# Chunked attention feeding a mixture of experts: the transpose of the later tiles' attention weights moved from TensorE to VectorE and ScalarE

## The chip, the cores and the metric

One core of a Trainium2 chip runs the program. The time is device microseconds of one execution, and the time of a kernel is the median of its runs; lower is better.

## The reference, cut to what matters

Attention works within chunks of 64 tokens, head by head; its output is the input of four experts, whose outputs are added with normalized weights.

```python
q_c, k_c, v_c = (a.reshape(B, H, nc, 64, 64) for a in (q, k, v))     # B = H = 8, S = 576
scores = np.matmul(q_c, k_c.transpose(0, 1, 2, 4, 3)) / 8
attn = np.exp(scores - np.max(scores, axis=-1, keepdims=True))
attn = attn / (np.sum(attn, axis=-1, keepdims=True) + 1e-09)
x = np.matmul(attn, v_c)            # to (4608 tokens, 512)
p = domain_probs / (domain_probs.sum(-1, keepdims=True) + 1e-09)
for e in range(4):
    out += p[:, e:e + 1] * (np.maximum(x @ w1[e], 0.0) @ w2[e])      # 512 -> 1024 -> 512
```

Everything is in float32.

## The kernel before, in words

The 4608 tokens are 36 tiles of 128. The first four tiles form a block of their own (startup, then the plain passes); the other 32 form four pairs of 512-token blocks, eight tiles to a pair. The experts are worked in eight passes (four experts by two halves of the hidden layer): a plain pass over the first block, then passes over the first pair, then "later passes" over the other pairs. The big products split each float32 operand into a high and a low part and add three products (L465, 512 columns a matmul); for the pairs a scheme with seven instead of eight block products saves some of them, at the price of sums of blocks (Factors, Tokens, Scaled). In a later pass the hidden products (g and h) and the output products (a and b of the pass before) are woven in the order of WOVEN, L1181.

The attention of a later tile is worked beside these products, some passes before its block is needed. One tile is 128 tokens: two chunks c by eight heads. Its steps are:
- a_scores (L135): 16 matmuls of 64x64 into psa, two PSUM banks that belong to attention alone. TensorE's array has four quadrants (64 rows by 64 columns); the chunk c sets the half of the rows, the head's parity the half of the columns, and the loop of quarters (L125) goes round all four.
- a_softmax (L145): VectorE takes the maximum and subtracts it (L185, L187), ScalarE takes exp (L190).
- a_weights (L149): VectorE sums, inverts and multiplies (L193 to L198) into e in SBUF.
- a_transpose (L156): TensorE transposes e in four matmuls of 128x128 (L160) into bank 0 of psa, and one ScalarE copy brings it to pt in SBUF (L162).
- a_values (L164): 16 matmuls of 64x64 with v as weights and pt streamed (L169), into the other half of psa.
- a_copy (L174): ScalarE copies the result into xraw (L178).

a_next (L218) issues a tile's values, then the next tile's scores, the copy, and the loads of the next v and of q and k after it; v_in and qk_in have one buffer each, so a load waits until TensorE has read the old one.

When a step is issued is set by hand. For the first pair, the generator attention (L200) yields a step at a time and Beside (L1005) spreads the steps evenly over the products of the plain passes; for the second pair over those of the first pair's passes. In the plain passes an idle step stands between weights and transpose (rest = 1), so there are 41 steps for a pair there, and 33 for the second pair. For the last two pairs, attend (L1197) adds the steps after given products of WOVEN: places EARLY (6, 9, 11) or LATE (17, 21, 24) for weights, transpose and a_next, by the table TILES, five EARLY and three LATE tiles to a pair. deferred (L504) holds work that issue (L1022) emits after the next product. Each engine works its instructions in the order of issue.

The startup has its own functions for its four tiles; they don't change.

Of the kernel before, what the change touches and what calls it, by code (L numbers as in the profile page):

```python
# [8 lines left out]
F32 = mybir.dt.float32  # L9
# [6 lines left out]
P = 128  # L16
C = 64
SUB = 512
NT = SUB // P
HG = 4  # L20
GT = 2
NK = 4
# [2 lines left out]
WAITS = {"loads": 6, "softmax": 6, "copy": 3}  # L25
PAIR = 2
N_RAW = 6


@with_exitstack  # L30
def chunk_attention_moe(ctx: ExitStack, tc: tile.TileContext, qk, v, v0, dp, w1, w2, out):
# [10 lines left out]
    nc = tc.nc  # L42
# [3 lines left out]
    n_pass = 2 * n_exp  # L46
# [5 lines left out]
    att = ctx.enter_context(tc.tile_pool(name="att", bufs=1))  # L52
# [54 lines left out]

    st = {}  # L110
    xraw = {}

# [7 lines left out]
    def a_load_v(t):  # L120
        s = st[t]
        s["v"] = load.tile([P, 2 * HG, C], F32, name="v_in")
        nc.sync.dma_start(out=s["v"], in_=v[t - NT])

    def quarters():  # L125
        for j in range(HG):
            for c in range(2):
                for odd in range(2):
                    yield j, slice(c * C, (c + 1) * C), c, slice(odd * C, (odd + 1) * C), odd

    def blocks(i):

        return psa[:, :, i * HG * C : (i + 1) * HG * C].rearrange("p c (j k) -> p c j k", k=C)

    def a_scores(t):  # L135
        s = st[t]
        s["sc"] = blocks(0)
        for j, rows, c, half, odd in quarters():
            g, h = divmod(2 * j + odd, HG)
            nc.tensor.matmul(  # L140
                s["sc"][half, c, j], lhsT=s["x"][rows, g, 0, h], rhs=s["x"][rows, g, 1, h],
                start=True, stop=True,
            )

    def a_softmax(t):  # L145
        less_max(st[t]["sc"])
# [2 lines left out]
    def a_weights(t):  # L149

        s = st[t]
        s["e"] = att.tile([P, HG, 2, C], F32, name="e")
        z = psa[:, 0, HG * C : HG * C + 2 * HG].rearrange("p (c j) -> p c j", c=2)
        a_norm(s["e"].rearrange("p j c k -> p c j k"), s["sc"], z)

    def a_transpose(t):  # L156
        s = st[t]
        ps = psa[:, 0].rearrange("p (j q) -> p j q", q=P)
        for j in range(HG):
            nc.tensor.transpose(ps[:, j], s["e"][:, j].rearrange("p c k -> p (c k)"), ident)  # L160
        s["pt"] = att.tile([P, HG, P], F32, name="pt")
        nc.scalar.copy(out=s["pt"], in_=ps)  # L162

    def a_values(t):  # L164

        s = st.pop(t)
        av = blocks(1)
        for j, rows, c, half, odd in quarters():
            nc.tensor.matmul(  # L169
                av[half, c, j], lhsT=s["v"][rows, 2 * j + odd], rhs=s["pt"][rows, j, half],  # L170
                start=True, stop=True,
            )

    def a_copy(t):  # L174
        pair, i = divmod(t - NT, PAIR * NT)
        if i == 0:
            xraw[pair] = xpool.tile([P, NK, PAIR * SUB], F32, name="xraw")
        nc.scalar.copy(  # L178
            out=xraw[pair][:, :, i * P : (i + 1) * P].rearrange("p j (c q) -> p c j q", c=2), in_=blocks(1)
        )  # L180


    def less_max(a):
# [13 lines left out]
        r = r.unsqueeze(len(a.shape) - 1).broadcast_to(a.shape)  # L197
        nc.vector.tensor_tensor(out=e, in0=a, in1=r, op=ALU.mult)  # L198

    def attention(pair, rest):  # L200

        first = (1 + pair * PAIR) * NT
        last = first + PAIR * NT
        a_load(first)
        yield
        a_next(None, first)
        for t in range(first, last):  # L210
            for step in (a_softmax, a_weights, *(rest * [None]), a_transpose):
                yield
                if step:
                    step(t)
            yield
            a_next(t, t + 1 if t + 1 < last else None)
# [287 lines left out]
    deferred = []  # L504
# [274 lines left out]
        s, j = divmod(i, NT)  # L779
        nc.tensor.transpose(out_ps, acc[pair + 1, m + NK * s][:, j * P : (j + 1) * P], ident)  # L780

    B = 32

    def put_out(pair, m, s, stage):

        t = (1 + pair * PAIR + s) * SUB
# [218 lines left out]
    class Beside:  # L1005


        def __init__(self, pair, n, rest):
            self.steps = attention(pair, rest)
            self.rate, self.due = ((4 + rest) * PAIR * NT + 1) / n, 0.5  # L1010

        def load(self):

# [183 lines left out]
    def attend(at, pair, places, i):  # L1197
        t = (1 + pair * PAIR) * NT + i
        after = t + 1 if i + 1 < PAIR * NT else None
        if i == 0:  # L1200
            add(at, 13, lambda: a_next(None, t))
            add(at, 14, lambda: a_softmax(t))
        add(at, places[0], lambda: a_weights(t))
        add(at, places[1], lambda: a_transpose(t))
        add(at, places[2], lambda: a_next(t, after))
        if after:
            add(at, places[2] + 1, lambda: a_softmax(after))
# [182 lines left out]
        by_halves(steps["b"])  # L1390

    with tc.manual_schedule():
        beside = [Beside(0, (n_pass - 3) * 2 * NK, 1), Beside(1, (n_pass - 1) * 26 - 4, 0)]
# [57 lines left out]
```

## Time and profile before

| what | value |
|---|---|
| median of 3 runs | 1506.08 us (1505.98 to 1506.42) |
| the profiled execution | 1506.8 us |
| its span, first to last instruction | 1504.9 us |
| TensorE busy | 1497.4 us (100%) |
| VectorE busy | 927.9 us (62%) |
| ScalarE busy | 564.2 us (37%) |
| GpSimd busy | 871.6 us (58%) |
| SyncE's DMA queue | 65.4% of 16 engines' span |

PE is TensorE's matmuls, PEld its weight loads, DVE is VectorE, ACT ScalarE, POOL GpSimd, SP the engine that issues the DMAs. A row of a timeline gives the start, the duration, the engine, the source line, the operation, what it writes and reads, and a count of merged instructions; in brackets the idle time before it and who ended it. Matmuls are pipelined, so their durations overlap: the time that one takes from the stream is read from start to start.

### The profile page before, as it was taken

The page shows a single profiled execution, that of the slowest core. Times are in us where ns is not written, and L with a number is a line of the kernel's source. Part 1 is how long each engine was busy: PE and PEld are TensorE (multiplying, and loading weights), DVE is VectorE, ACT ScalarE, POOL GpSimd, SP SyncE. Part 2 cuts the span into 40 slices and gives each one's busy share as a digit, 9 for nine tenths or more (in the row PEclk, how much of TensorE's full clock was granted, in tenths as well). Part 3 has the DMA queues.
Part 4 walks back from the last instruction along what each step waited for, and adds up shares of the span by engine and source line. Part 5 has one row for each costly group of instructions (what it writes and reads, how often), then busy time and mean ns, then how long its engine had stood idle before and what let it go on. Part 6 is the DMA issues. An engine that isn't in the chain of part 4 may idle for free.

```text
span 1504.9 us, 23273 instructions
## 1 busy us (share of the span) xinstructions
PE 1497.4 (100%) x8779; PEld 1231.3 (82%) x8779; DVE 927.9 (62%) x1306; ACT 564.2 (37%) x983; POOL 871.6 (58%) x666
## 2 busy tenths in 40 slices
PE   9999999999999999999999999999999999999998
PEld 7888888888888888888888888888888888888887
DVE  5453554445444466666776886667667966666666
ACT  3343444344444334333333434333333433323322
POOL 2443577677757616555565755555557655555555
PEclk9999999999999999999999999999999999999999
DMA  6353349886767576666675779666666696666665
GB/s 198 127 156 124 110 152 313 275 272 217 240 232 237 197 266 218 223 211 217 201 221 186 218 204 284 204 222 218 206 198 199 188 232 233 198 199 201 202 195 155
DMA packets 197775, 314.16 MB, mean 209 GB/s; under 512 B 53776, under 2 KB 113952, under 8 KB 197664
## 3 DMA queue, kind: packets, MB, share of 16 engines
q1 hardware_dynamic: 197664, 312.68, 65.4%
q8 instruction: 69, 1.13, 0.3%
q14 instruction: 42, 0.34, 0.1%
HBM read 244.39 MB, written 68.23 MB: 208 GB/s over the span
## 4 chain that ended last, share of the span: by engine, by line
PE 99%; DMA 0%; SPq 0%; DVE 0%; ACT 0%; issue 0%
PE A L465 49%; PE C L465 29%; PE B L465 16%; PE psa L169 1%; PE psa L140 1%; PE psa L160 1%; DMA xraw<-in_qk 0%; PE C L906 0%; PE B L857 0%; PE A L837 0%; SPq L821 0%; PE A L857 0%; PE B L843 0%; PE psa L837 0%; PE psa L843 0%; PE C L1357 0%
## 5 line engine op out<-in xcount | busy, mean ns | idle before, releaser
L647 POOL TENSOR_TENSOR hfl<-wraw,hfh 128x512 fp32r<-128x512 f32 x288 | 374.3, 1315 | 211.3 <-ACT hfh L644 209.5
L465 PE MATMUL A<-xh,wf 128*128 128x512 f32 (+1 forms) x1104 | 379.3, 389 | 0.0
L465 PE MATMUL A<-hfh,wf 128*128 128x512 f32 (+1 forms) x768 | 270.0, 393 | 0.0
L644 ACT CAST hfh<-wraw 128x512 fp32r<-128x512 f32 x288 | 176.5, 622 | 212.2 <-DVE wraw L638 60.7
L465 PEld LDWEIGHTS A<-xh,wf 128*128 128x128 f32 x1104 | 206.8, 188 | 43.3
L527 ACT COPY s<-A 128x512 f32<-128x512 f32 x192 | 112.9, 588 | 328.9 <-PE A L465 328.0
L465 PE MATMUL A<-xl,wf 128*128 128x512 f32 (+1 forms) x552 | 213.7, 388 | 0.0
L465 PE MATMUL C<-xh,wf 128*128 128x512 f32 (+1 forms) x600 | 203.9, 388 | 0.7 <-ACT xh L278 0.7
L465 PEld LDWEIGHTS A<-hfh,wf 128*128 128x128 f32 x768 | 144.1, 188 | 31.2 <-DVE acc L694 1.2
L694 DVE TENSOR_TENSOR acc<-A,acc 128x512 f32<-128x512 f32 x174 | 118.9, 684 | 72.0 <-PE A L465 71.5
L465 PE MATMUL A<-hfl,wf 128*128 128x512 f32 x384 | 149.4, 389 | 0.0
L465 PE MATMUL C<-hfh,wf 128*128 128x512 f32 x384 | 133.7, 389 | 0.0
L281 POOL TENSOR_TENSOR hfl<-wraw,hfh 128x512 fp32r<-128x512 f32 x64 | 85.9, 1370 | 80.3 <-ACT hfh L278 80.3
L465 PEld LDWEIGHTS C<-xh,wf 128*128 128x128 f32 x600 | 111.5, 188 | 23.8 <-ACT xh L278 0.8
L465 PE MATMUL B<-xh,wf 128*128 128x512 f32 (+1 forms) x376 | 125.2, 384 | 0.0
L281 POOL TENSOR_TENSOR wf<-wraw,wf 128x512 fp32r<-128x512 f32 x70 | 91.5, 1328 | 54.7 <-ACT wf L278 54.5
L465 PEld LDWEIGHTS A<-xl,wf 128*128 128x128 f32 x552 | 103.5, 188 | 21.0
L465 PE MATMUL C<-xl,wf 128*128 128x512 f32 (+1 forms) x300 | 114.7, 385 | 0.0
L638 POOL TENSOR_TENSOR wf<-wraw,wf 128x512 f32<-128x512 f32 x23 | 29.7, 1292 | 144.4 <-DVE wf L632 144.4
L694 DVE TENSOR_TENSOR acc<-C,acc 128x512 f32<-128x512 f32 x90 | 62.2, 691 | 52.9 <-PE C L465 47.3
L647 POOL TENSOR_TENSOR hfl<-wf,hfh 128x512 fp32r<-128x512 f32 x48 | 71.2, 1483 | 37.0 <-ACT hfh L644 36.7
L465 PEld LDWEIGHTS C<-hfh,wf 128*128 128x128 f32 x384 | 72.1, 188 | 15.0
(186 smaller groups left out, 2710.0 us busy)
## 6 DMA issues: line engine op xcount, KB each, us to landing
wf<-w SPq DMA_DIRECT2D x336, 512.0 KB, 4.2
wraw<-in_w SPq DMA_DIRECT2D x128, 256.0 KB, 3.9
w<-wf SPq DMA_DIRECT2D x112, 256.0 KB, 4.7
qk_in<-in_qk SPq DMA_DIRECT2D x32, 512.0 KB, 5.4
v_in<-in_v SPq DMA_DIRECT2D x32, 256.0 KB, 4.5
w<-hfl SPq DMA_DIRECT2D x32, 256.0 KB, 2.7
w<-hfh SPq DMA_DIRECT2D x32, 256.0 KB, 2.9
w<-hfh SPq DMA_DIRECT2D x48, 128.0 KB, 2.7
```

The costliest lines, as they stand in the source:

```text
L140: nc.tensor.matmul(s["sc"][half, c, j], lhsT=s["x"][rows, g, 0, h], rhs=s["x"][rows, g, 1, h], start=True, stop=True,)
L160: nc.tensor.transpose(ps[:, j], s["e"][:, j].rearrange("p c k -> p (c k)"), ident)
L169: nc.tensor.matmul(av[half, c, j], lhsT=s["v"][rows, 2 * j + odd], rhs=s["pt"][rows, j, half], start=True, stop=True,)
L281: eng.tensor_tensor(out=t[1], in0=src, in1=t[0].bitcast(F32), op=ALU.subtract)
L465: nc.tensor.matmul(out, lhsT=lhs(k, a), rhs=rhs(k, b), start=first and i == 0, stop=last and i == len(parts) - 1, skip_group_check=not (fi ...
L527: nc.scalar.copy(out=t, in_=self.a)
L638: (eng or nc.vector).tensor_tensor(out=self.values[place, k], in0=self.values[a, k], in1=self.values[b, k], op=op)
L644: nc.scalar.copy(out=self.part(name, 0)[:, k], in_=self.values[name, k])
L647: (eng or nc.gpsimd).tensor_tensor(out=self.part(name, 1)[:, k], in0=self.values[name, k], in1=self.part(name, 0)[:, k].bitcast(F32), op=A ...
L694: nc.vector.tensor_tensor(out=acc[key], in0=src, in1=acc[key], op=ALU.add)
```

## The change

The weights of a later tile are no longer transposed by TensorE. VectorE's transpose works on blocks of 32x32 and leaves every block in its place, so a 64x64 matrix comes out with its four blocks transposed one by one and the two off the diagonal in each other's place. a_transpose is now this one instruction, from e to the place in PSUM where the scores stood. A new step, a_place, brings it to pt: one ScalarE copy of everything, then four copies that each move blocks of 32 partitions from the other 32 partitions of the same half.

The scores are laid out for it. The weights of a head must end in the half of the partitions in which its values' matmul wants them, so the output half of a score matmul is now that of its later use (half), with heads assigned by c ^ half; v is loaded in three transfers instead of one, the second and third with the halves of the tokens swapped; the output copy becomes two, one of them with the two banks exchanged. In quarters the innermost loop is now the half: for scores it is the half of the columns, for values that of the rows.

In the plain passes the transpose is issued together with the weights, and the placing in the step after, through deferred, behind that step's product; an empty step follows. In the first pair's passes transpose and placing are steps of their own, so both pairs now have 41 steps. In attend, the transpose follows the weights at places[0], and the placing has the transpose's old place.

```diff
 def a_load_v(t):
-    nc.sync.dma_start(out=s["v"], in_=v[t - NT])
+    to, of = (a.rearrange("p (g i h) d -> p g i (h d)", g=2, i=2) for a in (s["v"], v[t - NT]))
+    nc.sync.dma_start(out=to[:, :, 0], in_=of[:, :, 0])
+    for half in range(2):
+        rows, other = slice(half * C, (half + 1) * C), slice((1 - half) * C, (2 - half) * C)
+        nc.sync.dma_start(out=to[rows, :, 1], in_=of[other, :, 1])
 def quarters():
-    for j in range(HG):
-        for c in range(2):
-            for odd in range(2):
-                yield j, slice(c * C, (c + 1) * C), c, slice(odd * C, (odd + 1) * C), odd
+    for g in range(2):
+        for c in range(2):
+            for odd in range(2):
+                for half in range(2):
+                    yield c, half, 2 * g + odd, HG * g + 2 * (c ^ half) + odd
 def a_scores(t):
-    s["sc"][half, c, j], lhsT=s["x"][rows, g, 0, h], rhs=s["x"][rows, g, 1, h],
+    q, k = (s["x"][of_half(c), head // HG, x, head % HG] for x in range(2))
+    nc.tensor.matmul(s["sc"][of_half(half), c, slot], lhsT=q, rhs=k, start=True, stop=True)
 def a_transpose(t):
-    ps = psa[:, 0].rearrange("p (j q) -> p j q", q=P)
-    for j in range(HG):
-        nc.tensor.transpose(ps[:, j], s["e"][:, j].rearrange("p c k -> p (c k)"), ident)
-    s["pt"] = att.tile([P, HG, P], F32, name="pt")
-    nc.scalar.copy(out=s["pt"], in_=ps)
+    nc.vector.transpose(st[t]["sc"], st[t]["e"])
+def a_place(t):
+    s["pt"] = att.tile([P, 2, HG, C], F32, name="pt")
+    nc.scalar.copy(out=s["pt"], in_=s["sc"])
+    for half in range(2):
+        for i in range(2):
+            here, there = (slice(half * C + k * B, half * C + (k + 1) * B) for k in (i, 1 - i))
+            nc.scalar.copy(
+                out=s["pt"][there, :, :, i * B : (i + 1) * B],
+                in_=s["sc"][here, :, :, (1 - i) * B : (2 - i) * B],
+            )
 def a_values(t):
-    av[half, c, j], lhsT=s["v"][rows, 2 * j + odd], rhs=s["pt"][rows, j, half],
+    av[of_half(slot % 2), half, head // 2], lhsT=s["v"][of_half(half), head],
+    rhs=s["pt"][of_half(half), c, slot], start=True, stop=True,
 def a_copy(t):
-    nc.scalar.copy(out=xraw..., in_=blocks(1))
+    nc.scalar.copy(out=to[:, :, 0::2], in_=av[:, :, 0::2])
+    nc.scalar.copy(out=to[:, :, 1::2], in_=av[:, ::-1, 1::2])
 def attention(pair, close):
-    for step in (a_softmax, a_weights, *(rest * [None]), a_transpose):
+    if close:
+        steps = (a_softmax,), (a_weights, a_transpose), (lambda t: deferred.append(lambda: a_place(t)),), ()
+    else:
+        steps = (a_softmax,), (a_weights,), (a_transpose,), (a_place,)
 class Beside:
-    self.rate, self.due = ((4 + rest) * PAIR * NT + 1) / n, 0.5
+    self.rate, self.due = (5 * PAIR * NT + 1) / n, 0.5
 def attend(at, pair, places, i):
-    add(at, places[0], lambda: a_weights(t))
-    add(at, places[1], lambda: a_transpose(t))
+    add(at, places[0], lambda: a_weights(t), lambda: a_transpose(t))
+    add(at, places[1], lambda: a_place(t))
```

ScalarE's order at the first tile that the plain passes work, before (pt is the transposed weights, psa attention's PSUM banks, hfh a hidden part, wf a split weight):

```order
L278 CAST wf_825<-wraw 128x2x256
L162 COPY pt<-psa 128x512
L278 CAST wf_848<-wraw 128x2x256
L278 CAST wf_851<-wraw 128x2x256
L178 COPY xraw<-psa 128x2x4x64
```

And after:

```order
L497 ACTIVATE hfh_796<-B_813 128x512
L175 COPY pt<-psa 128x512
L179 COPY pt<-psa 32x8x32 x4
L303 CAST wf_834<-wraw 128x2x256
L303 CAST wf_851<-wraw 128x2x256
L303 CAST wf_854<-wraw 128x2x256
L200 COPY xraw<-psa 128x2x2x64
L201 COPY xraw<-psa 128x2x2x64
```

Five copies stand where one stood, and one weight split earlier, right behind the hidden part's activation; the output copy is two.

PE's order at an early tile of a later pass, before (the last products of g7, then a7, g4 and a_next):

```order
L465 MATMUL A_6150<-xh_5427,wf_6134 128x512
L160 MATMUL psa<-ident,e 128x128 x4
L465 MATMUL A_6141<-hfh_6029,wf_6109 128x512
...
L465 MATMUL A_6150<-xl_5505,wf_6134 128x512
L465 MATMUL A_6150<-xh_5504,wf_6134 128x512
L169 MATMUL psa<-pt,v_in 64x64 x16
L140 MATMUL psa<-qk_in 64x64 x16
```

And after:

```order
L490 MATMUL A_6220<-xh_5491,wf_6204 128x512
L490 MATMUL A_6211<-hfh_6096,wf_6179 128x512
...
L490 MATMUL A_6220<-xl_5569,wf_6204 128x512
L490 MATMUL A_6220<-xh_5568,wf_6204 128x512
L189 MATMUL psa<-pt,v_in 64x64 x16
L154 MATMUL psa<-qk_in 64x64 x16
```

The four transposes are gone; values and scores stand where they stood. On ScalarE the placing follows the same copy of A as the copy to pt did:

```order
L552 COPY s_6319<-A_6220 128x512
L175 COPY pt<-psa 128x512
L179 COPY pt<-psa 32x8x32 x4
L200 COPY xraw<-psa 128x2x2x64
L201 COPY xraw<-psa 128x2x2x64
```

No other instruction has come between that copy and the output's.

More of the change, by code (lines that the diff above doesn't have):

```diff
@@ L27 @@
 N_RAW = 6
+B = 32
 @with_exitstack
@@ L122, in a_load_v, with of_half @@
         s["v"] = load.tile([P, 2 * HG, C], F32, name="v_in")
-        nc.sync.dma_start(out=s["v"], in_=v[t - NT])
+        to, of = (
+            a.rearrange("p (g i h) d -> p g i (h d)", g=2, i=2) for a in (s["v"], v[t - NT])
+        )
[3 more added lines that the diff above has]
+            nc.sync.dma_start(out=to[rows, :, 1], in_=of[other, :, 1])
     def quarters():
-        for j in range(HG):
+        for g in range(2):
             for c in range(2):
                 for odd in range(2):
-                    yield j, slice(c * C, (c + 1) * C), c, slice(odd * C, (odd + 1) * C), odd
+                    for half in range(2):
+                        yield c, half, 2 * g + odd, HG * g + 2 * (c ^ half) + odd
+    def of_half(i):
+        return slice(i * C, (i + 1) * C)
     def blocks(i):
@@ L137, in a_scores @@
         s["sc"] = blocks(0)
-        for j, rows, c, half, odd in quarters():
-            g, h = divmod(2 * j + odd, HG)
-            nc.tensor.matmul(
-                s["sc"][half, c, j], lhsT=s["x"][rows, g, 0, h], rhs=s["x"][rows, g, 1, h],
-                start=True, stop=True,
-            )
+        for c, half, slot, head in quarters():
+            q, k = (s["x"][of_half(c), head // HG, x, head % HG] for x in range(2))
+            nc.tensor.matmul(s["sc"][of_half(half), c, slot], lhsT=q, rhs=k, start=True, stop=True)
     def a_softmax(t):
@@ L167, in a_values @@
         av = blocks(1)
-        for j, rows, c, half, odd in quarters():
+        for c, half, slot, head in quarters():
             nc.tensor.matmul(
-                av[half, c, j], lhsT=s["v"][rows, 2 * j + odd], rhs=s["pt"][rows, j, half],
-                start=True, stop=True,
+                av[of_half(slot % 2), half, head // 2], lhsT=s["v"][of_half(half), head],
+                rhs=s["pt"][of_half(half), c, slot], start=True, stop=True,
             )
@@ L177, in a_copy @@
             xraw[pair] = xpool.tile([P, NK, PAIR * SUB], F32, name="xraw")
-        nc.scalar.copy(
-            out=xraw[pair][:, :, i * P : (i + 1) * P].rearrange("p j (c q) -> p c j q", c=2), in_=blocks(1)
-        )
+        to = xraw[pair][:, :, i * P : (i + 1) * P].rearrange("p j (c q) -> p c j q", c=2)
+        av = blocks(1)
+        nc.scalar.copy(out=to[:, :, 0::2], in_=av[:, :, 0::2])
+        nc.scalar.copy(out=to[:, :, 1::2], in_=av[:, ::-1, 1::2])
     def less_max(a):
@@ L198, in a_norm, with attention @@
         nc.vector.tensor_tensor(out=e, in0=a, in1=r, op=ALU.mult)
-    def attention(pair, rest):
+    def attention(pair, close):
         first = (1 + pair * PAIR) * NT
@@ L210, in attention @@
         for t in range(first, last):
-            for step in (a_softmax, a_weights, *(rest * [None]), a_transpose):
+            if close:
+                steps = (a_softmax,), (a_weights, a_transpose), (lambda t: deferred.append(lambda: a_place(t)),), ()
+            else:
+                steps = (a_softmax,), (a_weights,), (a_transpose,), (a_place,)
+            for some in steps:
                 yield
-                if step:
+                for step in some:
                     step(t)
@@ L1005, in chunk_attention_moe, with __init__ @@
     class Beside:
-        def __init__(self, pair, n, rest):
-            self.steps = attention(pair, rest)
-            self.rate, self.due = ((4 + rest) * PAIR * NT + 1) / n, 0.5
+        def __init__(self, pair, n, close):
+            self.steps = attention(pair, close)
+            self.rate, self.due = (5 * PAIR * NT + 1) / n, 0.5
         def load(self):
```

9 lines of the change are left out of this document (5 added, 4 removed).

## The prediction

> **What bounds the kernel now.** I read the page first: the busy times, the clock and the chain that ended last.
>
> ```profile
> PE 1497.4 (100%) x8779; PEld 1231.3 (82%) x8779; DVE 927.9 (62%) x1306; ACT 564.2 (37%) x983; POOL 871.6 (58%) x666
> ...
> PEclk9999999999999999999999999999999999999999
> ...
> PE 99%; DMA 0%; SPq 0%; DVE 0%; ACT 0%; issue 0%
> ```
>
> TensorE (PE) is the chain, 99% of it, at a full clock; all other engines have idle time. So a microsecond taken from PE's stream is a microsecond of the span as long as nothing that PE waits for comes late, and work added elsewhere costs nothing unless it makes PE wait. A busy PE may hide stalls, so I read its timeline at the first transposed tile.
>
> ```profile
> 55.27 0.61 PE L465 MATMUL B<-xh,wf 128*128 128x512 f32 x2
> 55.72 0.39 PE L465 MATMUL B<-xl,wf 128*128 128x512 f32 x1
> 55.95 0.40 PE L465 MATMUL B<-xh,wf 128*128 128x512 f32 x1
> 56.18 0.60 PE L160 MATMUL psa<-ident,e 128*128 128x128 f32 x4
> 56.54 0.48 PE L465 MATMUL C<-hfh,hfh 128*128 128x512 f32 x1
> 56.85 0.40 PE L465 MATMUL C<-hfl,hfh 128*128 128x512 f32 x1
> ```
>
> The first column is the start. From 55.27 to 55.95 three matmuls of 512 columns begin, so one takes 0.227 us. Without the four transposes of L160 the second C matmul would begin at 55.95 + 2 x 0.227 = 56.40; it begins at 56.85. The transposes cost 0.45 us, and nothing is idle around them: they are pure PE time.
>
> **The change part by part.** *Removed: the transposes.* The group row gives their number.
>
> ```profile
> L160 PE MATMUL psa<-ident,e 128*128 128x128 f32 x128 | 19.2, 273 | 0.0
> ```
>
> 128 are 32 tiles of four, and 32 x 0.45 = 14.3 us leave PE's stream (14.4 at the upper rounding). The column of idle time before them is 0.0, so no wait goes with them.
>
> *Reordered: scores and values.* Each tile keeps its 16 score and 16 value matmuls of 64x64.
>
> ```profile
> 59.17 0.39 PE L465 MATMUL C<-hfh,hfl 128*128 128x512 f32 x1
> 59.48 0.69 PE L169 MATMUL psa<-pt,v_in 64*64 64x64 f32 x32
> 60.00 0.65 PE L140 MATMUL psa<-qk_in 64*64 64x64 f32 x32
> 60.58 0.50 PE L465 MATMUL C<-hfh,hfh 128*128 128x512 f32 x1
> ...
> 16.42 1.15 PE L837 MATMUL psa<-xraw 64*64 64x64 f32 x32
> 17.41 1.10 PE L857 MATMUL B<-s,qk_in 64*64 64x64 f32 x32
> ```
>
> The loop of before goes round the four quadrants of the array (half of the rows by half of the columns), and 16 matmuls, 32 records, take 60.00 - 59.48 = 0.52 us. The startup's scores (L837) go back and forth between two quadrants and take 17.41 - 16.42 = 0.99. So time is the number of matmuls by the number of quadrants at work. The new values still go round all four: 0.52. The new scores do four matmuls on the two quadrants of one half of the rows, then four on the other two. Each of the four gets four matmuls as before; only the order is less even. The floor is 0.52; the ceiling is 0.99, only two at work throughout. I take 0.52: with two records to a matmul, four quadrants are full only if TensorE already begins later matmuls past one that waits for its quadrant. In strict order the price is between: a matmul holds its quadrant for 0.52 / 4 = 0.13, and the new order fills five such turns (2, 4, 4, 4, 2 matmuls) where the old one fills four: +0.13 us a tile, 4.2 us in all.
>
> The Trainium skill, "TensorE: Matmul & The Clock Gate", Part 3, "The mechanism", says that packed matmuls start and end in program order, "strict FIFO, no reordering". By that rule the sum would be 4.2 us less gain; the trace of before neither shows the order of two records on one quadrant nor settles it.
>
> *Added on VectorE: one block transpose a tile*, from e in SBUF into the scores' place in PSUM. The first row is of the view of tile pt (min/median/max in ns), the others are VectorE's and PE's timelines at a tile of a later pass.
>
> ```profile
> L797 DVE STREAM_TRANSPOSE pt<-acc x8: 697/701/712, 881.7 to 1229.8; 128x512 f32<-128x512 f32 x8
> ...
> 623.63 0.69 DVE L198 TENSOR_TENSOR e<-psa,z 128x512 f32<-128x512 f32 x1
> 624.57 0.69 DVE L694 TENSOR_TENSOR acc<-A,acc 128x512 f32<-128x512 f32 x1 [0.24 <-PE A L465]
> 625.92 0.69 DVE L694 TENSOR_TENSOR acc<-C,acc 128x512 f32<-128x512 f32 x1 [0.67 <-PE C L465]
> ...
> 627.10 0.60 PE L160 MATMUL psa<-ident,e 128*128 128x128 f32 x4
> 627.45 0.48 PE L465 MATMUL A<-hfh,wf 128*128 128x512 f32 x1
> ```
>
> The nearest operation takes 0.70 us, SBUF to SBUF; the same engine's multiply from PSUM takes 0.69, so the target in PSUM should change little. 32 x 0.70 = 22 us on an engine that is 62% busy. In a later pass it comes between L198 and the first L694: that add begins at 623.63 + 0.69 + 0.70 = 625.02 instead of 624.57, and the 0.67 idle before the next add swallows the 0.45. The bank that the first add frees is written again by the product at 627.45, over 1.7 us after the late end. Price: none. If the transpose took 1.4 us, the two adds would end 0.5 us later still, and PE would still not wait.
>
> The Trainium skill, "VectorE: DVE Perf Modes", "Rules for kernel authors", speaks against the swap: a 128x128 transpose should use TensorE where PSUM will do. By length alone the rows agree with it, 0.45 us on PE against 0.70; but the rule does not ask which engine is the bound, and here VectorE's time is free while TensorE's is not.
>
> *Added on ScalarE: the placing*, which is the risk. One copy of 128x512 becomes that copy and four of 32 partitions by 256 elements, and PE's values wait for the last. First the groups by form (busy us, mean ns, idle before), then timelines: ScalarE and PE in the same later pass, ScalarE in a plain pass.
>
> ```profile
> L162 ACT COPY pt<-psa 128x512 f32<-128x512 f32 x32 | 18.8, 589 | 20.5 <-PE psa L160 20.5
> ...
> L1345 ACT COPY s<-A 128x256 f32<-128x256 f32 x1 | 0.4, 372 | 0.3 <-PE A L1376 0.3
> L103 ACT COPY s<-B 128x128 f32<-128x128 f32 x1 | 0.3, 266 | 2.9 <-PE B L102 2.9
> L103 ACT COPY s<-B 16x128 f32<-16x128 f32 x1 | 0.2, 250 | 0.0
> ...
> 627.29 0.59 ACT L527 COPY s<-A 128x512 f32<-128x512 f32 x1 [2.43 <-PE A L465]
> 627.78 0.59 ACT L162 COPY pt<-psa 128x512 f32<-128x512 f32 x1
> 631.62 0.59 ACT L178 COPY xraw<-psa 128x512 f32<-128x512 f32 x1 [3.25 <-PE psa L140]
> ...
> 630.40 0.69 PE L169 MATMUL psa<-pt,v_in 64*64 64x64 f32 x32
> ...
> 56.38 0.60 ACT L472 ACTIVATE hfh<-B 128x512 fp32r<-128x512 f32 x1 [2.07 <-PE B L465]
> 56.88 0.61 ACT L278 CAST wf<-wraw 128x512 fp32r<-128x512 f32 x1
> ```
>
> 16 or 128 partitions cost the same (250 and 266 ns), so the length along the partition counts: 256 elements, 0.37 us. Consecutive copies overlap by 0.10 (627.29 + 0.59 against 627.78). End to end the five take 0.59 + 4 x 0.37 = 2.07 us; with the overlaps of the last three, 1.77. The first small one waits for the large one, whose output it overwrites in part; I take 1.8.
>
> The room: in a later pass's early tile the placing follows the copy of L527, which ends at 627.88, while the block transpose was done at 625.02. The values begin at 630.40, now 0.45 sooner because the transposes before them are gone, 629.95. That is 2.07 us, some 2.0 after a hand-over. Ten tiles are of this kind (places 6, 9, 11; five in each of two pairs). In the plain passes the placing now stands two steps ahead of the values, behind L472 of a hidden product, which ends at 56.98 where the values come at 59.48 - 0.45 = 59.03: 2.0 us again, for five tiles. So 15 tiles have 2.0 us for 1.8: no wait. At the upper end, 2.07 plus a hand-over between the first two, 0.1 x 15 = 1.5 us. The six late tiles (places 17, 21, 24) have a further step of room. In the first pair's passes the steps of attention are spread anew (41 instead of 33 over the same products), so eight placings land elsewhere.
>
> ```profile
> 170.00:510.00 340.00, 340.00 (x1979) 279.67 (x1978) 159.81 (x227) 146.86 (x261) 243.13 (x186) 1.00 0.71 235
> ```
>
> There (a stretch of the busy times by window; columns: PE, PEld, DVE, ACT, POOL busy) ScalarE is busy 147 of 340 us and PE all of them. A placing that lands ahead of an urgent copy may cost up to its own added 1.2 us, eight times at most 10, but with ScalarE over half idle I expect none or one: 0 to 1 us, and take 0. The output copy (L178) becomes two of 256, 0.74 for 0.59; what follows it waits for later work anyway.
>
> *Added on the DMA queue:* the values' load becomes three transfers with runs of 512 bytes.
>
> ```profile
> v_in<-in_v SPq DMA_DIRECT2D x32, 256.0 KB, 4.5
> ...
> 631.15 0.33 SPq L123 DMA_DIRECT2D v_in<-in_v  x1
> 631.62 0.38 SPq L118 DMA_DIRECT2D qk_in<-in_qk  x1
> 635.90 34.82 SPq L370 DMA_DIRECT2D wf<-w  x14
> 671.05 0.33 SPq L123 DMA_DIRECT2D v_in<-in_v  x1
> ...
> 690.55 0.33 SPq L123 DMA_DIRECT2D v_in<-in_v  x1
> ```
>
> Two further issues of 0.33 move the queries' load behind them by 0.7 us, and the queue's next load comes four microseconds later. The data lands in 4.5 us (the first row, of the DMA issues) and is used by the next tile's values, behind which the next load is issued: 19.5 us later here (690.55 - 671.05), 39.9 at most. Even if landing doubled, nothing waits.
>
> **The sum.** The profiled execution took 1506.8 us (span 1504.9 and 1.9 around it), 0.7 above the median of 1506.08. 1506.8 - 14.3 + 0 + 0 = 1492.5; against the median 1491.8. I give 1491.9, a tenth for the placing.
>
> **The rivals.**
> 1. *The score order binds*: strict order, +0.13 x 32 = 4.2 us: 1496.1. For it: the new order puts four matmuls in a row on two quadrants. Against it: two records to a matmul already run with all four full.
> 2. *The placing overruns a little*: at 0.45 us for a small copy, 0.59 + 4 x 0.45 = 2.4, 0.4 us late in 15 tiles, 6 us: 1498. For it: the margin is 0.2 us, and the runs of 32 elements are shorter than any in the rows. Against it: the row of 256 elements.
> 3. *Two quadrants only*: +0.47 x 32 = 15 us eats all: 1506.9, no change; the change then moves TensorE's time from transposes to scores. Against it: the other two quadrants' work is only four matmuls behind.
> 4. *Slower: placing becomes the bound.* PE waits for ScalarE once in each tight tile. It decides when 15 x (placing - 2.0) passes 14.3, a placing of 2.95 us, that is small copies of 0.59, as long as full ones. At 0.8 each it is 3.8 us, 27 us lost: 1519. For it: no row has 32 partitions written to other partitions. Against it: nothing in the rows makes 256 elements dearer than 512.
>
> **How the numbers follow.** The forecast has 0.68, rival 1 0.13, rival 2 0.11, rival 3 0.04, rival 4 0.04. The low end is 14.4 saved and 0.5 of scatter, 1491.2; the high end takes in rival 1 and the lower part of rival 2, 1496.6, and leaves out the rest, under 0.2. A difference of 0.2% (3 us) is about what a measurement of this kernel can tell from none: the forecast and the first two rivals are faster, 0.92; rival 3 is the same, 0.04; rival 4 slower, 0.04.
>
> **What would show it.** Right: no transposes of weights on PE; 0.227 us from matmul to matmul across the place where they stood; values after scores still 0.5 us apart; scores from their first to the next product 0.58 as now (60.58 - 60.00); the copies of 32 partitions near 0.37; no idle time on PE before values that ends with ScalarE. Wrong: scores of 0.7 (rival 1) or 1.0 (rival 3); an idle PE before values (rivals 2 and 4); or a PE wait for VectorE's adds or a weight load, which I priced at nothing.

## The result, and the profile after

The changed kernel took 1494.87 us in the median of four runs (1494.08 to 1495.03), the kernel before 1506.03 us in four runs beside it: a ratio of 0.9925, with a 95% interval of 0.9908 to 0.9942. That is 11.2 us less; the prediction was 14.2 less, and its range (1491.2 to 1496.6) holds the result. By the spans of the profiled executions, 1504.9 and 1493.1, it is 11.8. The startup differs by a microsecond or two from profile to profile (the first score of a later tile begins between 42.7 and 44.8 us), so where a microsecond counts the time from that score to the end is used below: 1460.3 us before, 1448.3 after, 12.0 less. It has one value for each kernel, from its profiled execution; how far it would scatter over more executions is not known.

The page's first and fourth parts after the change:

```profile
PE 1484.4 (99%) x8650; PEld 1220.0 (82%) x8651; DVE 946.0 (63%) x1338; ACT 611.1 (41%) x1143; POOL 870.8 (58%) x666
...
PE 90%; issue 3%; POOL 3%; DMA 2%; SPq 1%; DVE 0%; ACT 0%; POOLq 0%; ACTq 0%
```

TensorE's busy time fell by 13.0 us, ScalarE's rose by 47, VectorE's by 18. The second line looks as if TensorE were no longer the bound. It is: it is busy 1484.4 of 1493.1 us, and the account below, from the starts of its matmuls, finds the whole gain there. The chain is followed from a waiting instruction to whoever released it. At two stalls of PE (at 443 and 472 us, shown below) it leaves PE and runs back through other engines and transfers, to 316 us from the first and to 460 from the second. These 140 us are the 9% that PE lost in that line, for two waits of 0.4 us. Read the busy share and the starts first.

TensorE's timeline in a later pass, at the place where the transposes stood and then at the same tile's values and scores:

```profile
622.54 0.39 PE L490 MATMUL A<-hfh,wf 128*128 128x512 f32 x1
622.76 0.39 PE L490 MATMUL A<-xh,wf 128*128 128x512 f32 x1
622.99 0.39 PE L490 MATMUL A<-xl,wf 128*128 128x512 f32 x1
...
623.90 0.39 PE L490 MATMUL A<-xh,wf 128*128 128x512 f32 x1
624.25 0.69 PE L189 MATMUL psa<-pt,v_in 64*64 64x64 f32 x32
624.77 0.70 PE L154 MATMUL psa<-qk_in 64*64 64x64 f32 x32
625.40 0.50 PE L490 MATMUL C<-xh,wf 128*128 128x512 f32 x1
...
663.38 0.39 PE L490 MATMUL A<-xh,wf 128*128 128x512 f32 x1
663.79 0.69 PE L189 MATMUL psa<-pt,v_in 64*64 64x64 f32 x32
```

Three things are read from starts. Where the transposes were, a product now follows a product every 0.227 us (622.54, 622.76, 622.99). The scores take 625.40 - 624.77 = 0.63 us until the next product, where before they took 0.58. And the values begin 0.35 us after the last product in the first tile and 0.41 in the second (663.38 to 663.79), where before it was 0.31 (59.17 to 59.48): there is a small wait before them.

ScalarE's timeline at the second of these tiles, and its group row, show who ends it:

```profile
661.14 0.59 ACT L552 COPY s<-A 128x512 f32<-128x512 f32 x1 [2.42 <-PE A L490]
661.63 0.59 ACT L175 COPY pt<-psa 128x512 f32<-128x512 f32 x1
662.25 1.49 ACT L179 COPY pt<-psa 32x256 f32<-32x256 f32 x4
```

```profile
L179 ACT COPY pt<-psa 32x256 f32<-32x256 f32 x128 | 46.6, 364 | 2.1
```

A small copy takes 0.364 us, as forecast (0.37), but four of them take 1.49, 4 x 0.37: they do not overlap. The placing runs from 661.63 to 663.74, 2.11 us; the values begin 0.05 later. What TensorE's weight loads waited for, in us in total, times, longest:

```profile
PEld psa L189 <- ACT pt L179: 6.1, 15, 0.4
PEld psa L189 <- issue: 3.5, 10, 0.4
```

The second row stands where PE goes from products of 128x512 to the values of 64x64, which every tile pays: 0.35 each. The first has 6.1 / 15 = 0.41, so ScalarE's share is some 0.05 us in each of 15 tiles (0.04 in eleven, 0.09 in four), 0.8 us. They are the fifteen that the prediction had named as tight.

VectorE's transpose (the view of tile psa: min/median/max in ns) and the loads of v (the DMA issues: KB, us to landing):

```profile
L169 DVE STREAM_TRANSPOSE psa<-e x32: 715/727/728, 54.8 to 1096.3; 128x512 f32<-128x512 f32 x32
```

```profile
v_in<-in_v SPq DMA_DIRECT2D x32, 128.0 KB, 3.9
v_in<-in_v SPq DMA_DIRECT2D x64, 64.0 KB, 3.4
```

0.727 us where 0.70 was forecast, and loads that land sooner than the old one (4.5): nothing waits for either.

What the prediction priced at nothing shows in the first pair's passes, where the steps of attention were spread anew. TensorE's timeline at the two longest new stalls:

```profile
442.68 0.39 PE L490 MATMUL A<-xh,wf 128*128 128x512 f32 x1
443.29 0.50 PE L490 MATMUL C<-xh,wf 128*128 128x512 f32 x1 [0.23 <-DVE B L559]
443.63 0.39 PE L490 MATMUL C<-xl,wf 128*128 128x512 f32 x1
...
471.79 0.39 PE L490 MATMUL A<-xh,wf 128*128 128x512 f32 x1
472.33 0.50 PE L490 MATMUL A<-xh,wf 128*128 128x512 f32 x1
```

From 442.68 to 443.29 is 0.61 us instead of 0.227, and the next step is 0.34: 0.50 lost, with 0.11 of it in starting again. At the second place 471.79 to 472.33 is 0.54, and with the same restart it loses 0.42. VectorE's timeline ahead of the first, and ScalarE's at the second, say why:

```profile
441.94 0.69 DVE L219 TENSOR_TENSOR e<-psa,z 128x512 f32<-128x512 f32 x1
442.55 0.69 DVE L559 TENSOR_TENSOR B<-C,s 128x512 f32<-128x512 f32 x1
```

```profile
471.19 0.58 ACT L211 ACTIVATE psa<-psa 128x512 f32<-128x512 f32 x1 [3.88 <-DVE psa L208]
471.68 0.59 ACT L552 COPY s<-A 128x512 f32<-128x512 f32 x1
```

At 442 the add that frees bank C (L559) stands behind the attention's weights; at 471 the copy that frees bank A (L552) stands behind the attention's exp. Neither is a new instruction: old steps of attention now land ahead of an urgent one. With a third place at 259 us (0.14) these are 1.06 us.

The account, from the first later score to the end: transposes 15.8 less (32 x 0.494, the working follows further down), scores 1.6 more (32 x 0.05), placing 0.8 more, new stalls 1.1 more: 12.3 less, against 12.0 measured. The starts also show where the other 0.3 is. Behind the scores the products run a little wider than 0.227 apart for some steps, as they do behind the transposes; over all tiles that adds up (without the first step of 0.34) to 0.79 us before and 1.14 after.

### The profile page after: what moved, and what is told of

The parts are those of the page before. It is cut to its first block, busy times and chain, and to the rows that moved or that the text cites. A ratio compares the mean times of both kernels' runs of the same rounds, so it can differ in the third digit from the quotient of the medians.

```text
span 1493.1 us, 23262 instructions
## 1 busy us (share of the span) xinstructions
PE 1484.4 (99%) x8650; PEld 1220.0 (82%) x8651; DVE 946.0 (63%) x1338; ACT 611.1 (41%) x1143; POOL 870.8 (58%) x666
## 4 chain that ended last, share of the span: by engine, by line
PE 90%; issue 3%; POOL 3%; DMA 2%; SPq 1%; DVE 0%; ACT 0%; POOLq 0%; ACTq 0%
PE A L490 45%; PE C L490 27%; PE B L490 15%; PE psa L189 1%; PE psa L154 1%; POOL hfl L306 1%; POOL ws L345 1%; DMA w<-hfh 1%; POOL wraw L345 1%; DMA w<-wf 1%; POOL wf L306 1%; SPq L381 1%; DMA wraw<-in_w 0%; PE C L929 0%; SPq L385 0%
## 5 line engine op out<-in xcount | busy, mean ns | idle before, releaser
L552 ACT COPY s<-A 128x512 f32<-128x512 f32 x192 | 112.5, 588 | 315.1 <-PE A L490 314.2
```

What stands on the lines that cost most here:

```text
L552: nc.scalar.copy(out=t, in_=self.a)
```

## The experiments

Unless it says otherwise, a kernel is the changed one with one edit. "From the first score" is the time from the first later score to the end in the profiled execution.

| kernel | median us (runs) | ratio to before | 95% interval | from the first score |
|---|---|---|---|---|
| changed | 1494.87 (4) | 0.9925 | 0.9908 to 0.9942 | 1448.3 |
| e1_round | 1492.93 (5) | 0.9915 | 0.9901 to 0.9928 | 1447.6 |
| e2_place_early | 1494.80 (5) | 0.9926 | 0.9913 to 0.9938 | 1449.3 |
| e3_row | 1518.70 (4) | 1.0085 | 1.0071 to 1.0099 | 1473.9 |
| e4_both | 1492.86 (4) | 0.9915 | 0.9901 to 0.9928 | 1447.0 |
| e5_pe_transposes | 1533.88 (4) | 1.0183 | 1.0168 to 1.0198 | 1488.4 |
| e6_copies_twice | 1517.99 (4) | 1.0079 | 1.0064 to 1.0094 | 1472.4 |
| e7_dve_twice | 1495.43 (4) | 0.9928 | 0.9913 to 0.9943 | 1449.8 |
| e8_before_order | 1507.94 (10) | 1.0014 | 1.0004 to 1.0023 | 1462.3 |
| e9_spread | 1493.79 (4) | 0.9918 | 0.9903 to 0.9932 | 1448.0 |
| e10_three | 1492.02 (4) | 0.9906 | 0.9892 to 0.9921 | 1446.1 |
| e11_transposes_twice | 1518.53 (4) | 1.0085 | 1.0068 to 1.0102 | 1473.4 |

### What the order of the scores costs: e1_round, e8_before_order, e3_row

The first puts the scores of the changed kernel back into rounds of four quadrants; nothing else differs from the order of quarters.

```diff
+    def score_order():
+        for g in range(2):
+            for odd in range(2):
+                for c in range(2):
+                    for half in range(2):
+                        yield c, half, 2 * g + odd, HG * g + 2 * (c ^ half) + odd
 def a_scores(t):
-        for c, half, slot, head in quarters():
+        for c, half, slot, head in score_order():
```

> The changed kernel with one edit: the 16 score matmuls of a tile go round the four quadrants again (the loop over the chunk c inside the loop over odd), layout and everything else as changed. Theory (the order of the score matmuls costs the 0.05 us by which scores grew, from 0.58 to 0.63 us to the next product): scores back to 0.58 in all 32 tiles, 32 x 0.05 = 1.6 us off 1494.9, so 1493.3. Rival (the new layout of scores over quadrants and banks costs it): scores stay at 0.63 and the time at 1494.9.

TensorE's timeline at the first later tile:

```profile
58.52 0.65 PE L161 MATMUL psa<-qk_in 64*64 64x64 f32 x32
59.10 0.50 PE L497 MATMUL C<-hfh,hfh 128*128 128x512 f32 x1
```

The scores are back at 59.10 - 58.52 = 0.58 us, and so in every tile: the 0.05 belongs to the order, not to the new layout. The median fell by 1.9, but from the first score only 0.7 is gained: of the 1.6 won, 0.9 is lost again in longer stalls of the first pair's passes (0.90 at 441, 0.37 at 217.6), where an earlier TensorE meets the same late copies and adds.

The second makes the opposite edit to the kernel before: its scores in the changed kernel's order of quadrants.

```diff
 def a_scores(t):
-        for j, rows, c, half, odd in quarters():
+        for j, rows, c, half, odd in score_order():     # for g, for c, for j in (2g, 2g + 1), for odd
```

> The kernel before with the score matmuls alone in the changed order over the quadrants: four on the two quadrants of one chunk, then four on those of the other; its layout, transposes and copies are kept. Theory (the order alone costs 0.05 us a tile): scores 0.63 to the next product instead of 0.58, 1505.4 + 1.6 = 1507.0. Rival (the layout costs it): 1505.4.

TensorE's timeline at the first later tile:

```profile
58.32 0.69 PE L147 MATMUL psa<-qk_in 64*64 64x64 f32 x32
58.94 0.50 PE L472 MATMUL C<-hfh,hfh 128*128 128x512 f32 x1
```

The scores take 0.62 to 0.63 us in all 32 tiles, as in the changed kernel. The time is 1507.94 against 1506.04: 1.9 us more, an interval of 1.0004 to 1.0023, and 2.0 more from the first score. Of these 1.5 are the scores and 0.5 the wider steps of the products behind them. The order alone costs what it costs in the changed kernel, and the theory of a dearer layout falls.

The third goes the other way: each quadrant's four matmuls in a row, `for c, for half, for g, for odd`.

> The changed kernel with the score matmuls of each quadrant in a row: four on the first quadrant, four on the second, and so on. Theory (TensorE begins later matmuls past those that wait for their quadrant, over some distance, and the new order costs 0.05 only because it stands near the edge of that): scores clearly below a strict order, between 0.6 and 1.2 us a tile, 1495 to 1513. Rival (strict order of whole matmuls, 13 turns of 0.13): 1.7 us for 16 scores, 1.17 more than now in 32 tiles, 1531.

TensorE's timeline at the first later tile:

```profile
59.10 1.49 PE L161 MATMUL psa<-qk_in 64*64 64x64 f32 x32
60.52 0.50 PE L497 MATMUL C<-hfh,hfh 128*128 128x512 f32 x1
```

The scores take 1.42 us, 0.84 more than in rounds; the kernel loses the whole gain and more (1518.70). In strict order the four rows of four would fill 13 turns of 0.13 us instead of four, 1.17 more. A cheaper turn does not save strict order: 0.84 for nine further turns is 0.09 each, and the changed order, with one further turn, would then cost 0.09 and not 0.05. The single records that the row above merges show it directly. Five of them begin 0.058 us apart, one at a time, and of the rest more than half begin in pairs, some 0.005 apart, though the first quadrant's four matmuls are eight records. So TensorE does begin matmuls past others that wait for their quadrant, but not far: in the changed order, where two stand in the way, little is lost; in rows, where three do, only a part of the 1.17 is saved. How far it reaches exactly was not measured.

### The placing: e2_place_early, e4_both, e6_copies_twice

The tight tiles get more room: the early tiles place one product sooner, and in the plain passes the placing is issued ahead of its step's product instead of behind it.

```diff
-                steps = (a_softmax,), (a_weights, a_transpose), (lambda t: deferred.append(lambda: a_place(t)),), ()
+                steps = (a_softmax,), (a_weights, a_transpose), (a_place,), ()
-    EARLY, LATE = (6, 9, 11), (17, 21, 24)
+    EARLY, LATE = (6, 8, 11), (17, 21, 24)
```

> The changed kernel with the placing issued one product sooner: after product 8 instead of 9 in the early tiles, and ahead of its step's product in the plain passes instead of behind it. Theory (15 tight tiles begin their values 0.04 to 0.09 us late because the five copies take 2.11 us in 2.0): no value waits for ScalarE any more, 0.8 us off, 1494.1; scores stay at 0.63. Rival (the late start is not the placing's, or the earlier copies push a more urgent ScalarE copy so that PE waits elsewhere): 1494.9 or more.

The waits of the weight loads of values for ScalarE's placing go from fifteen to one:

```profile
PEld psa L189 <- ACT pt L179: 0.4, 1, 0.4
```

and no time is won: 1494.80, and from the first score 1.0 more. TensorE's rows of the timeline of all engines in the plain passes show where it went:

```profile
57.30 0.40 PE L490 MATMUL C<-hfl,hfh 128*128 128x512 f32 x1
...
57.66 0.19 PEld L490 LDWEIGHTS C<-hfh,hfl 128*128 128x128 f32 x1 [0.40 <-DVE hfl L498]
...
58.09 0.62 PE L189 MATMUL psa<-pt,v_in 64*64 64x64 f32 x26
```

The placing now stands ahead of the copy of the hidden product (L497), VectorE's low part (L498) comes later, and the product that reads it waits: 0.36 instead of 0.227, and the values then start 0.43 after it. Two of the five plain tiles so lose 0.25 and 0.31 us where each had lost 0.04, and a stall of 1.04 us appeared at 257.8, where the weight load waits for a ScalarE copy (L552). Right on the cause, and of no use in the plain passes: a small wait was exchanged for larger ones. The ten early tiles show no such price; their values all begin 0.32 after the product.

e4_both is the two edits together.

> The changed kernel with both the round order of the scores and the earlier placing. Theory (the sum of before had two terms mis-sized, 1.6 us of score order and 0.8 us of late placing, and nothing else): both come off, 1494.9 - 1.6 - 0.8 = 1492.5, with no PE wait at values or scores left. Rival (something else took part of the 14.4 us of the transposes): 1493.5 or more, with the difference in another place.

1492.86: the scores are at 0.58 and no early tile waits, as expected, but it is hardly faster than e1_round (0.1 by the medians, 0.6 from the first score). Its profiled execution lost 3.3 us in stalls, where the changed kernel's lost 2.0; 0.8 of them are a weight load at 915 us that waits for its own DMA, which no edit touches. From the first score 1.3 of the forecast 2.4 came.

e6_copies_twice issues each small copy twice (the second repeats the work), 1.46 us more of ScalarE a tile.

```diff
+                for _ in range(2):
                     nc.scalar.copy(out=s["pt"][there, ...], in_=s["sc"][here, ...])
```

> The changed kernel with each of the four small copies of the placing done twice, so that the placing takes 4 x 0.365 = 1.46 us longer, 3.57 in all. Theory (15 tiles have 2.0 us of room, the others at least a product more): values wait 1.5 us in 15 tiles, 22 us, 1517; if further ScalarE copies come late, somewhat more. Rival (ScalarE's length is hidden but for the last hundredths): under 1500.

TensorE's and ScalarE's timelines at an early tile:

```profile
630.33 0.39 PE L491 MATMUL A<-xh,wf 128*128 128x512 f32 x1
632.26 0.69 PE L190 MATMUL psa<-pt,v_in 64*64 64x64 f32 x32 [1.54 <-ACT pt L180]
```

```profile
629.14 3.07 ACT L180 COPY pt<-psa 32x256 f32<-32x256 f32 x8
```

The values come 1.93 us after the product instead of 0.32: 1.6 lost, in the same fifteen tiles and next to nothing in the other seventeen; 15 x 1.6 = 24, against 23.1 by the medians and 24.0 from the first score. This is the fourth rival's mechanism: past 2.0 us of placing, and up to the 3.6 of this run, each further microsecond costs about 15. The changed kernel sits 0.1 us beyond that edge.

### VectorE's transpose: e7_dve_twice

```diff
 def a_transpose(t):
-        nc.vector.transpose(st[t]["sc"], st[t]["e"])
+        for _ in range(2):
+            nc.vector.transpose(st[t]["sc"], st[t]["e"])
```

> The changed kernel with VectorE's block transpose done twice, the second over the first, 0.73 us more on VectorE in each of 32 tiles. Theory (VectorE's transpose is hidden): 1494.9, within 0.5. Rival (part of the missing gain is VectorE's later adds, on which TensorE's banks wait): a microsecond or more for the 23 us, 1496 to 1505.

VectorE is busier by 22 us (968.1), PE by 0.7. Two of PE's new waits, from the timeline of its weight loads:

```profile
677.41 0.19 PEld L491 LDWEIGHTS A<-hfh,wf 128*128 128x128 f32 x1 [0.24 <-DVE acc L720]
...
917.61 0.19 PEld L491 LDWEIGHTS B<-hfh,wf 128*128 128x128 f32 x1 [1.22 <-DMA wf<-w]
```

1495.43, 0.6 more than the changed kernel, and 1.5 more from the first score (1449.8). Of the 1.5, 0.96 is the second wait, with 0.11 for the restart behind it: a weight load waits for its DMA. The same wait stands in kernels without the doubled transpose (0.81 in e4_both, 0.57 in e10_three), so that the transpose has a part in it is not shown. For the first wait it is: with the doubled transpose VectorE's adds (L720) come late at four places (677, 758, 995 and 1076 us), and PE loses 0.09 at each. So the rival is right in kind and by far too large: 0.36 us for 23. A single transpose, as in the changed kernel, is hidden; twice its length is hidden in all but four places. The prediction had said that PE would not wait even at 1.4 us; that holds at the tile that it read, not at these four.

### What the transposes had cost: e5_pe_transposes, e11_transposes_twice

The first gives the changed kernel four transposes of 128x128 on TensorE back, whose result nobody reads.

```diff
+    def a_idle_transposes(t):
+        e = st[t]["e"].rearrange("p c j k -> p (c j k)")
+        for j in range(HG):
+            to = psa[:, j // 2, HG * C + j % 2 * P : HG * C + (j % 2 + 1) * P]
+            nc.tensor.transpose(to, e[:, j * P : (j + 1) * P], ident)
-        add(at, places[1], lambda: a_place(t))
+        add(at, places[1], lambda: a_idle_transposes(t), lambda: a_place(t))
```

In the other passes they stand in the step after the placing, or in the placing's step ahead of it.

> The changed kernel, and beside it TensorE still does the four 128x128 transposes of e per tile at their old places, into the idle half of attention's banks; nobody reads them. Theory (the transposes cost 0.45 us and slow the next ten matmuls by 0.04 us in all, 15.8 us for 32 tiles, and they gave ScalarE 0.45 us more time before the values): +15.8 for the transposes, -0.8 because no value waits for the placing any more, 1509.9. Rival (only 0.45 us each): 14.4 - 0.8, 1508.5. Both see the matmul after the transposes 0.31 us from the next; the theory sees 0.235 instead of 0.227 from one matmul to the next behind them.

1533.88, far off both. The experiment was badly built: in the plain passes the idle transposes, which write the same tile of PSUM that the placing reads, waited for its copies, eight times.

```profile
PEld psa L175 <- ACT pt L185: 18.9, 8, 3.1
```

In the first pair's passes, too, PE stalled longer than in the changed kernel, 0.56 and 1.15 us at 470 and 472, behind a late copy of ScalarE and a late add of VectorE. The time then told of these waits and not of transposes. The transposes themselves can be read wherever they stand ahead of the placing, in the 24 tiles of the other passes: each costs what it cost in the kernel before, 0.59 us from product to product, 0.31 to the next, and ten steps of 0.232. In the later passes of the last two pairs, sixteen tiles take 522.77 us (617.36 to 1140.13) against 515.27 in the changed kernel, 7.5 more. The placing's waits in this stretch, some 0.55 in all, are gone meanwhile, so the account's 0.494 a tile would give 7.35; the rival (0.45 alone, less the same) would give 6.65.

The second takes the kernel before and doubles its transposes (the same four twice).

```diff
-        for j in range(HG):
+        for j in [*range(HG)] * 2:
             nc.tensor.transpose(ps[:, j], s["e"][:, j].rearrange("p c k -> p (c k)"), ident)
```

> The kernel before with the four transposes of TensorE done twice in a row, the second over the first. Theory (what the change removes: 4 x 0.109 us, and slower matmuls behind them only where the array comes back from them): four more cost 0.436 us each time, 14.0 us for 32 tiles, 1520.0, and the slowing of the product behind is paid once, as before. Rival (the slowing goes with the number of transposes): 15.8, 1521.8.

TensorE's timeline at the first transposed tile:

```profile
54.36 0.40 PE L465 MATMUL B<-xh,wf 128*128 128x512 f32 x1
54.60 1.04 PE L160 MATMUL psa<-ident,e 128*128 128x128 f32 x8
55.39 0.48 PE L465 MATMUL C<-hfh,hfh 128*128 128x512 f32 x1
55.70 0.40 PE L465 MATMUL C<-hfl,hfh 128*128 128x512 f32 x1
...
57.98 0.39 PE L465 MATMUL C<-hfh,hfl 128*128 128x512 f32 x1
```

From the last product to the second C product it is 55.70 - 54.36 = 1.34 us where it was 0.90: 0.44 for the further four, 14.0 us in all. But the ten products behind take 57.98 - 55.70 = 2.28, 0.228 each, where in the kernel before they take 59.17 - 56.85 = 2.32 (the prediction's rows). So the slower stride behind the transposes is not a price for each transpose: with eight of them it is gone. 14.0 less 32 x 0.04 is 12.7, and 12.5 was measured (13.1 from the first score); I had expected 14.

### A better version: e9_spread, e10_three

e9_spread puts the second pair back to four steps a tile (33 over the same products), with transpose and weights in one step.

```diff
-                steps = (a_softmax,), (a_weights,), (a_transpose,), (a_place,)
+                steps = (a_softmax,), (a_weights, a_transpose), (a_place,)
-            self.rate, self.due = (5 * PAIR * NT + 1) / n, 0.5
+            self.rate, self.due = ((4 + close) * PAIR * NT + 1) / n, 0.5
```

> The changed kernel with the second pair's attention spread as before over the first pair's passes: the transpose in the step of the weights, the placing in the old transpose's step, 33 steps instead of 41; the rest as changed. Theory (the new spread puts the weights ahead of an add of VectorE at 442, and exp ahead of a copy of ScalarE at 471, on which TensorE waits 0.50 and 0.42 us with what the clock-in of the next matmul adds, and 0.14 at 259): these stalls of the changed kernel's profile go, 1.1 us off, 1493.8. Rival (they come from the weights' loads and splits of those passes, whatever attention does): stalls of about a microsecond stay there, 1494.9.

The stalls at 259, 442 and 471 went, but others came at 231, 273 and 486: 1.6 us of stalls in place of 2.0. The median is 1.1 lower, from the first score only 0.3. So the three go with the spread, as forecast, and another spreading has its own. Their size is less certain than their place: with the spread of the changed kernel the stall near 442 is 0.50 there, 0.90 in e1_round, 0.19 in e7_dve_twice and not seen in e3_row.

e10_three takes together what had worked: e1's rounds, e2's edit of the early tiles alone, and e9's spread.

> The changed kernel with three edits: the round order of the scores, the placing of the early tiles after product 8 instead of 9, and the old spread of the second pair; the plain passes stay as changed. Theory (three terms priced at nothing were 1.6, 0.6 in the early tiles and 1.1): 1494.9 - 3.3 = 1491.6, below both kernels and below the forecast. Rival (the terms do not add, or the stalls move to another copy): 1493 or more.

TensorE's timeline at an early tile:

```profile
621.04 0.39 PE L497 MATMUL A<-xh,wf 128*128 128x512 f32 x1
621.36 0.69 PE L196 MATMUL psa<-pt,v_in 64*64 64x64 f32 x32
621.88 0.65 PE L161 MATMUL psa<-qk_in 64*64 64x64 f32 x32
622.45 0.50 PE L497 MATMUL C<-xh,wf 128*128 128x512 f32 x1
```

The values start 0.32 after the product, the scores take 0.57: both small losses are gone at this tile (the plain ones still wait 0.04). 1492.02 us, the lowest of all, 2.25 less than the changed kernel from the first score where 3.3 had been expected: the stalls of e9_spread at 231 and 273 are here too, and at 914 a weight load waits 0.57 for its DMA. The two intervals against the kernel before overlap (0.9892 to 0.9921, 0.9908 to 0.9942), so that this version is faster than the changed one rests on the traces, not on the medians alone.

## Why the prediction was right, and which terms were off

The direction, the mechanism and the range held: the gain is TensorE's time for the transposes, what replaced them is hidden or nearly so, and neither the slower rival nor that of no change came. The median is 3.0 us above the forecast. Four terms were off, by 2.0 net, and 0.3 are the wider steps behind the scores, which the sum did not have. A further 0.8 is the difference between 12.0 and the medians' 11.2: 0.2 is in the startup of the two profiled executions, and most of the rest comes from the kernel before, whose profiled execution took 1506.8 where its median is 1506.03. The forecast had allowed 0.1. Of the prediction's own signs of being right, two failed in small: the scores grew to 0.63, and PE was idle before values in the fifteen tight tiles.

- **The transposes: 14.3 forecast, 15.8 by the account.** The prediction read the 0.45 from the last product to the second one behind, and that is what they took. It stopped reading there. The next ten products ran 0.232 us apart instead of 0.227, another 0.044 us a tile (32 x 0.494 = 15.8). After the change that stride is 0.227, and e5's 24 tiles bear the sum out; that it does not grow with the number of transposes is shown by e11. Its cause stays open.
- **The order of scores: 0 forecast, 1.6 measured.** The step that failed is "I take 0.52", the floor. The first rival's mechanism was right in kind, a further turn for the less even order, and its price too high: 0.05 a tile, not 0.13. That is about one record and not a whole matmul: the startup's scores, 16 records on each of two quadrants in 0.99 us, put a record at 0.06. The Trainium skill's sentence that packed matmuls run in strict order without reordering ("TensorE: Matmul & The Clock Gate", Part 3, "The mechanism") would have given 0.13 here and 1.17 in e3; the runs show 0.05 and 0.84. Here the measurement decides: there is some passing over, of short reach.
- **The placing: 0 forecast, 0.8 measured.** Fifteen tight tiles with 2.0 us of room was right to the tile. Forecast at 1.8, the placing took 2.11: the overlap of 0.10, taken from two full-size copies, does not hold for the small ones. For the length the upper end, 2.07, was the better figure; its price, 1.5 us for all, was as far above the 0.8 as the forecast's 0 was below.
- **The respread of the first pair's steps: "0 to 1 us, and take 0"; 1.06 measured.** The prediction looked at the added placings. What made TensorE wait was none of them but old steps, the weights on VectorE and the exp on ScalarE, that land at other products than before.
- **VectorE's transpose and the loads of v: nothing forecast, nothing measured** (0.727 us for 0.70; 3.9 and 3.4 us to landing). Twice the transpose costs 0.36 us in four waits (e7).

The sum goes 14.3 to 15.8 on one side and 0 to 3.5 on the other: the largest term was taken too low, and every uncertain price at its lowest end. That the two errors partly cancel is luck: with 14.3 for the transposes and the other prices as they came, the median would have been some 1496.4, just inside the range.

## What to carry to other kernels

When the bound engine's work goes to engines with idle time, the gain is what its stream shows from start to start, read on until the stride is normal again; then count the tiles whose hand-over has little room, since each microsecond of overrun costs once for each of them. Steps that are spread evenly beside other work land elsewhere as soon as their number changes, so price all of them, not only the new ones. Where work is packed on the quadrants of the array, go round the quadrants one at a time: the order alone was worth 1.6 us here, and in a bad order 25.

## What the runs showed of the hardware that was not expected

**The clock after a wait.** In e5, TensorE's timeline and busy times by window (the columns are window, length, busy time of PE, PEld, DVE, ACT and POOL with counts, granted clock, DMA share, GB/s) at the first wait for the placing, and the busy times behind the second:

```profile
58.03 1.12 PE L175 MATMUL psa<-ident,e 128*128 128x128 f32 x4 [2.68 <-ACT pt L185]
...
59.37 0.63 PE L496 MATMUL C<-hfl,hfh 128*128 128x512 f32 x1
59.80 0.63 PE L496 MATMUL C<-hfh,hfl 128*128 128x512 f32 x1
```

```profile
59.40:63.50 4.10, 4.10 (x11) 3.23 (x10) 0.00 (x0) 0.26 (x1) 3.04 (x3) 0.50 0.00 0
```

```profile
79.20:84.00 4.80, 4.80 (x81) 3.94 (x82) 0.72 (x2) 2.46 (x5) 2.71 (x3) 1.00 0.26 75
```

After this wait of 2.7 us the granted clock is 0.50, and products come 0.43 us apart instead of 0.227. But it is not so after every such wait. Five in this run have PE idle for the same 2.7 us. Behind three of them, at 58, 114 and 166 us, the clock is at 0.50 for 3.4 to 6.8 us, which costs another 1.6 to 2.9 us; behind the two at 79 and 147 it stays at 1.00. What decides between them no run here shows. The waits of 0.04 to 1.6 us in the other kernels show nothing of the kind.

**Small copies on ScalarE.** 32 partitions by 256 elements take 0.364 us and do not overlap with each other, where a full-size copy behind another begins 0.10 before its end (661.14 + 0.59 against 661.63).

**A matmul's stride.** Behind four transposes the next ten products are 0.232 us apart, behind eight 0.228. It is no property of transposes: behind the scores, too, some five to ten steps are as wide (0.236 and 0.233 among them) before the stride is 0.227 again, and how many differs with how the scores end. No run here says why.
